# Weight pairs prepared in pieces, activations two items ahead, and a last pair without shared sums

## The chip, the cores and the metric

The kernel runs on one core of a Trainium2 chip. The metric is the device time of one execution in microseconds (us). A core has a matrix engine (TensorE, PE in the profile), a vector engine (VectorE, DVE), a scalar engine (ScalarE, ACT), GpSimd (POOL), and SyncE (SP), which here only starts transfers. Each works through its own instructions in the order in which they stand, and waits on semaphores for the others. Line numbers in this part and in the prediction (L714) are those of the kernel before.

## The reference

A transformer-like block on x of 2048 rows by 512 columns, all in float32. Six vectors of 512 come from a condition c. Then:

```
mod = (silu(c) @ w_mod)              # sa, ca, ga, sb, cb, gb
h = layernorm(x) * (1 + ca) + sa
x = x + ga * irfft2(rfft2(h) * (w_r + i w_i))
h = layernorm(x) * (1 + cb) + sb
a = mish(h @ w1 + b1)                # w1: 512 x 1376, mish(u) = u * tanh(softplus(u))
x = x + gb * (a @ w2)                # w2: 1376 x 512
```

## The kernel before

The work has four stages. Stages one and two do the forward transform, the product with the weights in the spectrum, and half of the way back. Stage three finishes the inverse transform, 16 row blocks of 128 rows each. The last stage is the MLP.

**Stage three** is a loop over s = 0 to 16, written out by hand: each engine gets its instructions in the order of the calls. A step has a column product (`p3_col`, L637 and L638, into a bank that ScalarE copies at L640), the row product of the step before (`p3_row`, L647, whose result VectorE adds to x at L650), and the statistics of that row block (`norm_sums`, L111 and L112). `norm_scale` (L116 and L117 on ScalarE, L124 and L129 on VectorE) turns the statistics of two or four row blocks into scales. Beside this the weights of the MLP are prepared. They are split into a high part in a shorter format and the rest, so that a product in float32 is made of three fast ones (`TERMS`). For w1: twelve pieces are loaded (L588), copied to the high part by ScalarE (L594) and subtracted by GpSimd (L595). For w2, in pairs t = 1 to 5 of 128 rows each, and a last odd piece t = 0 of 96 rows: `load_w2` (L673), `sum_w2` (GpSimd multiplies with the gate gb, L679, and forms four differences in `tsum`, L684), `split_w2` (ScalarE copies at L696, VectorE subtracts at L697). All of one function is called in one step; the table `prep` says in which. Pairs 4 and 5 are prepared after the loop, under the first MLP items.

**The MLP** goes over 8 blocks of two row blocks (b), each with 6 items (t). An item is the first product `up` (L714, 24 matmuls for a pair, 12 for t = 0, into one of two banks "A"), `mish` (ScalarE's Mish at L723, sums of halves on VectorE at L734, the high part `ah` by two copies of ScalarE at L740), `low` (the rest, `al`, VectorE at L746), and the second product `down` (L761; L755 for t = 0). For a pair, `down` multiplies a 2 x 2 scheme with 7 products of half size instead of 8; sums of weights (`tsum`) and of activations replace the eighth, and four of the results (`out_ps` banks 0, 3, 4, 5) are combined at the end of a block: `gather` copies them (L768), `chain` adds two of them up, `residual` adds banks 1 and 2 to x (L778), `spread` adds the combined ones (L783 to L787), `store` sends both row blocks out (L791). The tiles `ah` and `al` come from a pool with two buffers:

```
    act = ctx.enter_context(tc.tile_pool(name="act", bufs=2))
```

The next block's rows are normalised by `norm_pair` (ScalarE, L140) at t = 2, transposed by TensorE at t = 3 and 4 (`transpose_in`, L616, also into a bank "A") and split by `split_in` (L624 on ScalarE, L628 and L629 on VectorE). The step of item s is `up(s)`, `mish(s)`, `down(s - 1)`, `low(s)`.

Of the kernel before, what the change touches and what calls it, by code (L numbers as in the profile page):

```python
# [10 lines left out]
ALU = mybir.AluOpType  # L11

P = 128
# [12 lines left out]
LAST = (RAW[0], *SUM[0:3], RAW[1], RAW[2], SUM[3])  # L26
# [3 lines left out]
def tile_spectral_block(ctx: ExitStack, tc: tile.TileContext, x_d, w1_d, b1_d, w2_d,  # L30
# [645 lines left out]
    def sum_w2(t):  # L676
        rs = st["w2", t]
        for r in rs:
            nc.gpsimd.tensor_tensor(r, r, gbr[:r.shape[0]], op=ALU.mult)  # L679
        if t:  # L680
            u, v = rs
            for o, a, b in ((0, u[:, 256:], u[:, 0:256]), (1, v[:, 256:], tsum[:, 0]),
                            (2, v[:, 256:], u[:, 256:]), (3, v[:, 0:256], tsum[:, 1])):
                nc.gpsimd.tensor_tensor(tsum[:, o], a, b, op=ALU.subtract)  # L684

    def split_w2(t):
        rs = st.pop(("w2", t))
        hi, lo = w2[t]
        if t == 0:
            parts = [(rs[0], hi[:96], lo[:96])]  # L690
        else:
            flat = [w.rearrange("p e d -> p (e d)") for w in (hi, lo)]
            cut = ((rs[0][:, 0:256], 0, 256), (rs[1], 256, 768), (tsum.rearrange("p e d -> p (e d)"), 768, 1792))
            parts = [(r, flat[0][:, a:b], flat[1][:, a:b]) for r, a, b in cut]
        for r, h, l in parts:
            nc.scalar.copy(h, r)  # L696
            nc.vector.tensor_tensor(l, r, plain(h), op=ALU.subtract)  # L697
# [19 lines left out]
    def mish(g):  # L717
# [8 lines left out]
        if t == 0:  # L726
            parts = [(w[:rows, 0:256], slice(0, 2))]
        else:
# [19 lines left out]
    def down(g):  # L748
# [9 lines left out]
        for n, half, e, r in LAST if g == NB * NT - 1 else RAW + SUM:  # L758
            o = out[n][:, 0:256] if half is None else out[n][:, 256 * half:256 * half + 256]
            for i, (p, q) in enumerate(TERMS):  # L760
                nc.tensor.matmul(o, a[p][:, e], w2[t][q][:, r], start=(half is None and t == 1 and i == 0),  # L761
                                 stop=(t == 5 and i == 2 and (n, half) != (1, 0)))
# [13 lines left out]
    def residual(b):  # L776
        for n, ps in ((2 * b + 1, out_ps[b][1]), (2 * b, out_ps[b][2])):
            nc.vector.tensor_tensor(x[:, n, :], x[:, n, :], ps, op=ALU.add)  # L778

    def spread(b, ea, eb):  # L780
        p, q = done.pop(b)
        u, v = x[:, 2 * b + 1, :], x[:, 2 * b, :]
        ea.tensor_tensor(u, u, p, op=ALU.add)  # L783
        ea.tensor_tensor(v[:, 256:], v[:, 256:], p[:, 256:], op=ALU.add)
# [11 lines left out]
    def mlp(s):  # L796
        b, t = divmod(s, NT)
        nxt = 2 * b + 2 if b < NB - 1 else None
        if s < total:
            up(s)  # L800
# [197 lines left out]
```

## Time and profile before

| what | value |
|---|---|
| three runs | 427.13 us median (426.91 to 430.45) |
| profiled execution, its own time | 427.34 us |
| its span, first to last instruction | 425.3 us |
| mean granted clock of TensorE | 0.985 |
| busy: PE, DVE, ACT, POOL | 396.7, 259.7, 220.3, 145.8 us |
| from the first product of stage three to the last | 110.87 to 172.59 us |
| start of the last product, last start of an output transfer's pair | 415.42, 421.73 us |

The busy time of TensorE is an upper bound, since the ends of pipelined matmuls are modelled. What counts is where an engine that bounds a stage stands still, and who ended that. A row of the timeline has start, duration, engine, line, operation, output<-input, partitions x elements, the number of such instructions merged, and in brackets the idle time before it and who ended it.

### The profile page before, as it was taken

What the parts mean: (1) busy time and instruction counts of PE and PEld (TensorE: products, weight loads), DVE (VectorE), ACT (ScalarE), POOL (GpSimd) and SP (SyncE); (2) the same over time, 40 slices, a digit from 0 to 9 for tenths busy, and PEclk for the clock granted to TensorE, in tenths of its full rate; (3) what the DMA queues carried; (4) which work ended last, traced back from release to release, by engine and by line L of the source; (5) the groups of instructions that cost most, each with busy time, mean ns of one, the idle gap of its engine ahead of it and who ended that gap; (6) DMA issues with size and microseconds to landing.
All of it is one profiled execution on the core that took longest, in us unless ns stands there. A gap on an engine that the chain in (4) does not pass through costs nothing.

```text
span 425.3 us, 8110 instructions
## 1 busy us (share of the span) xinstructions
PE 396.7 (93%) x3161; PEld 384.1 (90%) x3161; DVE 259.7 (61%) x543; ACT 220.3 (52%) x495; POOL 145.8 (34%) x180
## 2 busy tenths in 40 slices
PE   9999899999977777899999999999999999999993
PEld 8888778899877776899999999999999999999993
DVE  2899949677166766779655455545644654563534
ACT  2677754577544443466464354454455553554431
POOL 0677625565075546415500500500500401303101
PEclk9999999999998969999999999999999999999998
DMA  8999652281203222010000100100100100100101
GB/s 300 379 337 363 219 208 75 76 324 50 74 18 117 66 99 62 26 51 2 17 34 2 46 5 2 51 1 2 52 2 0 51 2 0 51 2 0 51 2 49
DMA packets 20613, 34.72 MB, mean 82 GB/s; under 512 B 3680, under 2 KB 6528, under 8 KB 20192
## 3 DMA queue, kind: packets, MB, share of 16 engines
q1 hardware_dynamic: 20144, 33.68, 23.1%
q8 instruction: 25, 0.41, 0.4%
q10 hardware_dynamic: 432, 0.53, 0.4%
q14 instruction: 12, 0.10, 0.1%
HBM read 30.01 MB, written 4.19 MB: 80 GB/s over the span
## 4 chain that ended last, share of the span: by engine, by line
PE 64%; DVE 17%; ACT 6%; issue 5%; POOL 5%; DMA 2%; DVEq 0%; POOLq 0%; ACTq 0%
PE bank L714 26%; PE bank L761 20%; PE bank L455 3%; PE bank L755 3%; PE bank L501 3%; DVE st L111 3%; DMA buf<-in_B_w_dram 2%; POOL modr L684 2%; DVE ve L124 2%; POOL buf L679 2%; PE bank L488 2%; DVE buf L734 1%; PE bank L434 1%; DVE buf L226 1%; DVE buf L206 1%
## 5 line engine op out<-in xcount | busy, mean ns | idle before, releaser
L734 DVE TENSOR_TENSOR buf<-buf 128x128 f32<-128x128 f32 x160 | 52.2, 367 | 70.9 <-ACT buf L723 69.4
L723 ACT ACTIVATE buf<-bank,b1n 128x256 f32<-128x256 f32 (+1 forms) x88 | 37.3, 470 | 74.4 <-PE bank L714 74.4
L740 ACT CAST ah<-buf 128x512 fp32r<-128x512 f32 (+2 forms) x88 | 48.6, 552 | 38.7 <-DVE buf L734 37.1
L746 DVE TENSOR_TENSOR al<-buf,ah 128x512 fp32r<-128x512 f32 (+2 forms) x88 | 54.9, 624 | 10.0 <-ACT ah L740 10.0
L773 POOL TENSOR_TENSOR buf<-buf 128x256 f32<-128x256 f32 x7 | 5.2, 743 | 158.1 <-ACT buf L768 158.1
L714 PE MATMUL bank<-h2o,w1h 128*128 128x256 f32 (+1 forms) x352 | 52.8, 282 | 0.0
L714 PE MATMUL bank<-h,w1h 128*128 128x256 f32 (+1 forms) x352 | 52.7, 282 | 0.0
L714 PEld LDWEIGHTS bank<-h2o,w1h 128*128 128x128 f32 (+1 forms) x352 | 46.5, 186 | 0.3
L714 PEld LDWEIGHTS bank<-h,w1h 128*128 128x128 f32 (+1 forms) x352 | 46.4, 186 | 0.3
L761 PE MATMUL bank<-w2a,ah 128*128 128x256 f32 x168 | 36.8, 286 | 0.0
L761 PE MATMUL bank<-w2b,ah 128*128 128x256 f32 x168 | 36.3, 283 | 0.0
L647 PE MATMUL bank<-kiv,buf 128*128 128x128 f32 x128 | 19.3, 300 | 12.5 <-ACT buf L640 12.5
L647 PEld LDWEIGHTS bank<-kiv,buf 128*128 128x128 f32 x128 | 17.4, 211 | 13.5 <-ACT buf L640 13.5
L761 PEld LDWEIGHTS bank<-w2b,ah 128*128 128x128 f32 x168 | 28.2, 191 | 0.0
L761 PEld LDWEIGHTS bank<-w2a,ah 128*128 128x128 f32 x168 | 28.1, 191 | 0.0
L714 PE MATMUL bank<-h,w1l 128*128 128x256 f32 (+1 forms) x176 | 28.0, 282 | 0.0
L714 PE MATMUL bank<-h2o,w1l 128*128 128x256 f32 (+1 forms) x176 | 28.0, 282 | 0.0
L637 PE MATMUL bank<-kc,d 128*128 128x128 f32 x128 | 26.2, 288 | 0.5 <-ACT d L359 0.5
L638 PE MATMUL bank<-kc,d 128*128 128x128 f32 x128 | 26.0, 286 | 0.0
L233 PE MATMUL bank<-buf,mring 128*128 128x512 f32 x48 | 21.4, 445 | 4.2 <-DVE buf L226 1.9
L111 DVE BATCH_NORM_STATS2 st<-x 128x6 f32<-128x512 f32 x32 | 22.0, 688 | 3.8 <-DMA x<-in_A_x_dram 3.4
L595 POOL TENSOR_TENSOR w1l<-buf,w1h 128x512 fp32r<-128x512 f32 (+1 forms) x12 | 14.7, 1229 | 28.0 <-ACT w1h L594 28.0
(195 smaller groups left out, 1007.5 us busy)
## 6 DMA issues: line engine op xcount, KB each, us to landing
buf<-in_B_w_dram SPq DMA_DIRECT2D x18, 256.0 KB, 2.8
xring<-in_x_t_dram SPq DMA_DIRECT2D x16, 256.0 KB, 4.5
x<-in_A_x_dram SPq DMA_DIRECT2D x16, 256.0 KB, 4.8
wm<-in_w_mod_dram SPq DMA_DIRECT2D x16, 256.0 KB, 4.3
out_dram<-x SPq DMA_DIRECT2D x16, 256.0 KB, 2.0
mraw<-in_km_dram SPq DMA_DIRECT2D x16, 128.0 KB, 4.5
wqa<-in_w_q_dram SPq DMA_DIRECT2D x8, 256.0 KB, 4.4
wqb<-in_w_q_dram SPq DMA_DIRECT2D x8, 256.0 KB, 5.7
```

What stands on the lines that cost most here:

```text
L111: nc.vector.bn_stats(t, x[:, n, :])
L233: nc.tensor.matmul(pa, m[:, a, 0:128], g, start=(i == 0), stop=False)
L595: nc.gpsimd.tensor_tensor(w1l[:, k, lo:hi], r, plain(w1h[:, k, lo:hi]), op=ALU.subtract)
L637: nc.tensor.matmul(o, dj[:, 0:128], kc[0][:, n, :], start=True, stop=False)
L638: nc.tensor.matmul(o, dj[:, 64:192], kc[1][:, n, :], start=False, stop=True)
L647: nc.tensor.matmul(px[:, j * P:(j + 1) * P], e[:, j * P:(j + 1) * P], kiv[:, j, :], start=True, stop=True)
L714: nc.tensor.matmul(ps[:rows, 256 * e:256 * e + 256], w[:, k, f * P:f * P + rows], h[:, k, :], start=(i == 0), stop=(i == 11))
L723: nc.scalar.activation(w[:rows, c], ps[:rows, c], AF.Mish, bias=b1n[:rows, f:f + 1])
L734: nc.vector.tensor_tensor(o, p, q, op=op)
L740: nc.scalar.copy(h, r)
L746: nc.vector.tensor_tensor(l, r, h, op=ALU.subtract)
L761: nc.tensor.matmul(o, a[p][:, e], w2[t][q][:, r], start=(half is None and t == 1 and i == 0), stop=(t == 5 and i == 2 and (n, half) != (1, ...
```

## The change

- `sum_w2` becomes `gate_w2` (one tile at a time) and `sum_w2` (some of the differences); `split_w2` takes the raw part or the differences. For pairs 1, 2 and 3, starting at step s = 1, 6 and 11, the load stands at step s - 1, the two gate products at s and s + 1, the raw split and two differences at s + 2, the other two at s + 3, the split of the differences at s + 5. The order within a step and the steps of `norm_scale` and `norm_pair` are moved.
- `up(0)` stands at step 15 and `up(1)` at step 16 of stage three; `down` follows two items behind (`LAG = 2`). `norm_pair` moves to t = 3, the transpositions to t = 4 and 5 and ahead of `up`; the end of a block moves to t = 1.
- The last pair of the last block is multiplied plainly (8 products of half size, made as 4 of 512 columns, 12 matmuls), with raw weights that are loaded and gated once more. The shared sums are so complete one item earlier, and `finish` orders the end.

```
-LAST = (RAW[0], *SUM[0:3], RAW[1], RAW[2], SUM[3])
+LAG = 2
...
@@ -673,28 +673,40 @@
             nc.sync.dma_start(r, w2_d[f * P:f * P + rows, :])
             rs.append(r)
 
-    def sum_w2(t):
-        rs = st["w2", t]
-        for r in rs:
+    def gate_w2(t, *es):
+        for e in es:
+            r = st["w2", t][e]
             nc.gpsimd.tensor_tensor(r, r, gbr[:r.shape[0]], op=ALU.mult)
-        if t:
-            u, v = rs
-            for o, a, b in ((0, u[:, 256:], u[:, 0:256]), (1, v[:, 256:], tsum[:, 0]),
-                            (2, v[:, 256:], u[:, 256:]), (3, v[:, 0:256], tsum[:, 1])):
-                nc.gpsimd.tensor_tensor(tsum[:, o], a, b, op=ALU.subtract)
-
-    def split_w2(t):
-        rs = st.pop(("w2", t))
+
+    def sum_w2(t, *os):
+        u, v = st["w2", t]
+        for o in os:
+            a, b = ((u[:, 256:], u[:, 0:256]), (v[:, 256:], tsum[:, 0]),
+                    (v[:, 256:], u[:, 256:]), (v[:, 0:256], tsum[:, 1]))[o]
+            nc.gpsimd.tensor_tensor(tsum[:, o], a, b, op=ALU.subtract)
+
+    def split(h, l, r):
+        nc.scalar.copy(h, r)
+        nc.vector.tensor_tensor(l, r, plain(h), op=ALU.subtract)
+
+    def split_w2(t, sums):
         hi, lo = w2[t]
         if t == 0:
-            parts = [(rs[0], hi[:96], lo[:96])]
+            split(hi[:96], lo[:96], st.pop(("w2", 0))[0])
+            return
+        h, l = (w.rearrange("p e d -> p (e d)") for w in (hi, lo))
+        if sums:
+            split(h[:, 768:], l[:, 768:], tsum.rearrange("p e d -> p (e d)"))
         else:
-            flat = [w.rearrange("p e d -> p (e d)") for w in (hi, lo)]
-            cut = ((rs[0][:, 0:256], 0, 256), (rs[1], 256, 768), (tsum.rearrange("p e d -> p (e d)"), 768, 1792))
-            parts = [(r, flat[0][:, a:b], flat[1][:, a:b]) for r, a, b in cut]
-        for r, h, l in parts:
-            nc.scalar.copy(h, r)
-            nc.vector.tensor_tensor(l, r, plain(h), op=ALU.subtract)
+            u, v = st["w2", t]
+            split(h[:, 0:256], l[:, 0:256], u[:, 0:256])
+            split(h[:, 256:768], l[:, 256:768], v)
+
+    def plain_w2():
+        w2["plain"] = [w.rearrange("p e d -> p (e d)") for w in w2[1]]
+        h, l = w2["plain"]
+        for e, r in enumerate(st.pop(("w2", 5))):
+            split(h[:, 512 * e:512 * e + 512], l[:, 512 * e:512 * e + 512], r)
 
     def apply_gate():
         gb = bank("B")
@@ -725,6 +737,8 @@
         acts[g] = hi, lo
         if t == 0:
             parts = [(w[:rows, 0:256], slice(0, 2))]
+        elif g == total - 1:
+            parts = [(w, slice(0, 4))]
         else:
             u = buf("g2")
             a = w.rearrange("p (e s) -> p e s", s=P)
@@ -755,11 +769,19 @@
                     nc.tensor.matmul(out[n], a[p][:96, half], w2[0][q][:96], start=(i == 0), stop=False)
             return
         out = out_ps[b]
-        for n, half, e, r in LAST if g == NB * NT - 1 else RAW + SUM:
+        if g == total - 1:
+            for n, half in ((2, 0), (1, 1)):
+                for f in range(2):
+                    for i, (p, q) in enumerate(TERMS):
+                        nc.tensor.matmul(out[n], a[p][:, half + 2 * f], w2["plain"][q][:, 512 * f:512 * f + 512],
+                                         start=False, stop=(f == 1 and i == 2))
+            return
+        for n, half, e, r in RAW + SUM:
             o = out[n][:, 0:256] if half is None else out[n][:, 256 * half:256 * half + 256]
+            last = t == 5 or (half is None and g == total - 2)
             for i, (p, q) in enumerate(TERMS):
                 nc.tensor.matmul(o, a[p][:, e], w2[t][q][:, r], start=(half is None and t == 1 and i == 0),
-                                 stop=(t == 5 and i == 2 and (n, half) != (1, 0)))
+                                 stop=(last and i == 2 and (n, half) != (1, 0)))
 
     def gather(b):
         out = out_ps[b]
...
@@ -773,21 +795,29 @@
         eng.tensor_tensor(q[:, 0:256], q[:, 0:256], p[:, 0:256], op=ALU.add)
         eng.tensor_tensor(q[:, 256:], q[:, 256:], q[:, 0:256], op=ALU.add)
 
-    def residual(b):
-        for n, ps in ((2 * b + 1, out_ps[b][1]), (2 * b, out_ps[b][2])):
-            nc.vector.tensor_tensor(x[:, n, :], x[:, n, :], ps, op=ALU.add)
-
-    def spread(b, ea, eb):
-        p, q = done.pop(b)
+    def residual(b, rows=(1, 0)):
+        for r in rows:
+            n = 2 * b + r
+            nc.vector.tensor_tensor(x[:, n, :], x[:, n, :], out_ps[b][2 - r], op=ALU.add)
+
+    def rows_of(b):
+        p, q = done[b]
         u, v = x[:, 2 * b + 1, :], x[:, 2 * b, :]
-        ea.tensor_tensor(u, u, p, op=ALU.add)
-        ea.tensor_tensor(v[:, 256:], v[:, 256:], p[:, 256:], op=ALU.add)
-        eb.tensor_tensor(u[:, 256:], u[:, 256:], q[:, 0:256], op=ALU.add)
-        vv = v.rearrange("p (j d) -> p j d", j=2)
-        eb.tensor_tensor(vv, vv, q[:, 256:].unsqueeze(1).to_broadcast([P, 2, 256]), op=ALU.add)
-
-    def store(b):
-        for n in (2 * b + 1, 2 * b):
+        return (
+            lambda eng: eng.tensor_tensor(u, u, p, op=ALU.add),
+            lambda eng: eng.tensor_tensor(u[:, 256:], u[:, 256:], q[:, 0:256], op=ALU.add),
+            lambda eng: eng.tensor_tensor(v[:, 256:], v[:, 256:], p[:, 256:], op=ALU.add),
+            lambda eng: eng.tensor_tensor(v.rearrange("p (j d) -> p j d", j=2), v.rearrange("p (j d) -> p j d", j=2),
+                                          q[:, 256:].unsqueeze(1).to_broadcast([P, 2, 256]), op=ALU.add))
+
+    def spread(b):
+        chain(b, nc.gpsimd)
+        for fn in rows_of(b):
+            fn(nc.gpsimd)
+
+    def store(b, rows=(1, 0)):
+        for r in rows:
+            n = 2 * b + r
             nc.sync.dma_start(ov[:, n:n + 1, :], x[:, n:n + 1, :])
 
     total = NB * NT
@@ -796,31 +826,47 @@
     def mlp(s):
         b, t = divmod(s, NT)
         nxt = 2 * b + 2 if b < NB - 1 else None
-        if s < total:
-            up(s)
-        if t in (3, 4) and nxt:
-            transpose_in(nxt, t - 3)
-        parts = mish(s) if s < total else ()
-        if t == 2 and nxt:
+        if t in (4, 5) and nxt:
+            transpose_in(nxt, t - 4)
+        up(s)
+        if t in (4, 5) and nxt:
+            split_in(nxt, t - 4)
+        parts = mish(s)
+        if t == 3 and nxt:
             norm_pair(nxt)
-        down(s - 1)
-        if t == 0:
+        down(s - LAG)
+        if t == 1 and b:
             gather(b - 1)
-            if s == total:
-                chain(b - 1, nc.vector)
             residual(b - 1)
         low(parts)
-        if t in (3, 4) and nxt:
-            split_in(nxt, t - 3)
-        if t == 0:
-            if s < total:
-                chain(b - 1, nc.gpsimd)
-            spread(b - 1, nc.gpsimd, nc.vector if s == total else nc.gpsimd)
+        if t == 1 and b:
+            spread(b - 1)
             store(b - 1)
 
+    def finish():
+        b = NB - 1
+        down(total - 2)
+        gather(b)
+        own, ahead, far, both = rows_of(b)
+        chain(b, nc.vector)
+        far(nc.vector)
+        own(nc.gpsimd)
+        both(nc.vector)
+        down(total - 1)
+        residual(b, (0,))
+        store(b, (0,))
+        ahead(nc.vector)
+        residual(b, (1,))
+        store(b, (1,))
+
     apply_gate()
-    prep = {1: (load_w2, 1), 2: (sum_w2, 1), 3: (split_w2, 1), 4: (load_w2, 2), 5: (sum_w2, 2), 8: (split_w2, 2),
-            9: (load_w2, 3), 10: (sum_w2, 3), 11: (split_w2, 3), 12: (load_w2, 0), 13: (sum_w2, 0), 16: (split_w2, 0)}
+    prep = {s: [] for s in range(N2 + 1)}
+    for t, s in ((1, 1), (2, 6), (3, 11)):
+        for lag, fn, *args in ((-1, load_w2, t), (0, gate_w2, t, 0), (1, gate_w2, t, 1), (2, split_w2, t, False),
+                               (2, sum_w2, t, 0, 1), (3, sum_w2, t, 2, 3), (5, split_w2, t, True)):
+            prep[s + lag].append((fn, args))
+    prep[14].append((load_w2, (0,)))
+    prep[15].append((gate_w2, (0, 0)))
     for s in range(N2 + 1):
         if s < N2:
             p3_col(s)
@@ -828,37 +874,54 @@
             load_w1(s)
         if s >= 1:
             p3_row(s - 1)
+        if s in (3, 5):
+            norm_scale(s - 3, s - 1)
+        if s in (9, 13):
+            norm_scale(s - 5, s - 1)
+        if s == 15:
+            up(0)
+        if s == 16:
+            up(1)
         if s in (7, 8):
             transpose_in(0, s - 7)
+        if s >= 1:
+            norm_sums(s - 1)
         if 2 <= s < 14:
             split_w1(s - 2)
         if s in (8, 16):
             w2_space({8: 2, 16: 4}[s])
-        if s in prep:
-            prep[s][0](prep[s][1])
-        if s >= 1:
-            norm_sums(s - 1)
-        if s in (2, 4):
-            norm_scale(s - 2, s)
-        if s in (8, 12, 16):
-            norm_scale(s - 4, s)
-        if s == 4:
+        for fn, args in prep[s]:
+            fn(*args)
+        if s == 5:
             norm_pair(0)
         if s in (7, 8):
             split_in(0, s - 7)
-        if s == 16:
-            up(0)
-    low(mish(0))
+    norm_scale(N2 - 4, N2)
+    split_w2(0, False)
+    parts = mish(0)
+    low(parts)
+    parts = mish(1)
+    low(parts)
     load_w2(4)
-    sum_w2(4)
-    for s in range(1, total + 1):
+    gate_w2(4, 0, 1)
+    sum_w2(4, 0, 1, 2, 3)
+    for s in range(LAG, total):
         mlp(s)
-        if s == 2:
-            split_w2(4)
+        if s == 3:
+            split_w2(4, False)
+            split_w2(4, True)
             load_w2(5)
-            sum_w2(5)
-        if s == 4:
-            split_w2(5)
+            gate_w2(5, 0, 1)
+            sum_w2(5, 0, 1, 2, 3)
+        if s == 5:
+            split_w2(5, False)
+            split_w2(5, True)
+        if s == total - 5:
+            load_w2(5)
+            gate_w2(5, 0, 1)
+        if s == total - 3:
+            plain_w2()
+    finish()
 
 
 def _constants():
```

## The prediction

> **What bounds the kernel now.** I first read the busy time in four stretches: stage three (the inverse transform by columns and rows with the weights of the MLP prepared beside it), the first MLP items, the rest of the MLP, and the end. Columns: stretch, its length, then for each engine the busy time and the instructions, then the granted clock.
>
> ```profile
> 110.87:172.59 61.72, 49.19 (x392) 48.21 (x393) 37.93 (x72) 26.37 (x55) 33.99 (x32) 0.92 0.21 63
> 172.59:182.85 10.26, 9.03 (x69) 8.32 (x68) 7.61 (x17) 4.53 (x9) 4.37 (x5) 1.00 0.08 27
> 182.85:415.42 232.57, 232.11 (x1915) 230.17 (x1914) 128.11 (x289) 117.83 (x246) 46.06 (x48) 1.00 0.05 19
> 415.42:425.30 9.88, 2.97 (x23) 2.56 (x21) 4.41 (x8) 1.55 (x5) 1.94 (x2) 0.87 0.14 53
> ```
>
> The MLP is bound by TensorE: 232.11 of 232.57 us busy. Only there does every stall of TensorE count in full, and nothing that only makes another engine faster counts. TensorE loses time in stage three and in the 9.88 us from the start of the last product. The waits of stage three (waiter, who ended it; total, times, longest) say why:
>
> ```profile
> ACT rstd L116 <- DVE mv L112: 12.6, 5, 3.4
> PE bank L647 <- ACT buf L640: 12.5, 5, 4.7
> ACT w L696 <- POOL modr L684: 2.9, 1, 2.9
> ```
>
> The row product L647 waits for the copy L640, which stands on ScalarE behind the wide weight copy L696 (waiting for GpSimd's differences) or behind L116 (waiting for statistics that VectorE makes after the weights' low parts). A long wait costs twice, as the clock shows in stretches of 3.41 us:
>
> ```profile
> 129.24:132.65 3.41, 1.26 (x12) 1.07 (x10) 2.60 (x9) 1.97 (x5) 0.00 (x0) 1.00 0.69 219
> 132.65:136.06 3.41, 2.94 (x14) 2.94 (x15) 1.62 (x4) 1.93 (x4) 2.40 (x2) 0.50 0.09 19
> ...
> 146.30:149.71 3.41, 0.06 (x1) 0.00 (x0) 2.77 (x6) 0.93 (x4) 0.00 (x0) 1.00 0.20 53
> 149.71:153.13 3.42, 2.08 (x10) 2.08 (x10) 3.06 (x9) 2.67 (x6) 1.54 (x2) 0.50 0.00 0
> ...
> 159.95:163.37 3.42, 2.01 (x18) 1.81 (x17) 0.36 (x2) 1.10 (x2) 3.42 (x4) 1.00 0.00 0
> ```
>
> Each half-clock stretch follows one in which TensorE was busy 1.26 or 0.06 us; after 2.01 us there is none. So the limit lies between 37% and 59% of a stretch.
>
> **The change, part by part.**
>
> *Stage three.* Undisturbed, a step costs what lies between two row products:
>
> ```profile
> 117.23 1.06 PE L647 MATMUL bank<-kiv,buf 128*128 128x128 f32 x8
> ...
> 119.91 1.06 PE L647 MATMUL bank<-kiv,buf 128*128 128x128 f32 x8
> ```
>
> That is 2.68 us; 16 steps and two transpositions (0.35 us each, from 219.39 to 219.74 in the step shown below) make 43.6 us. The stage took 61.7, so 18.1 are lost. The first items (two first products, up(0) half-sized, one half-sized second product, another first product: 1.42 + 2.85 + 1.42 + 2.85 = 8.5 us) took 10.26: 1.7 more. In all 19.8 us can be won at most.
>
> The change spreads a weight pair over six steps: loads one step ahead, a gate product in each of two steps, narrow copies and two differences, two more differences, and the wide copy two steps later. That copy then finds its differences made, and the scale of the norms stands one step behind its statistics. GpSimd's work is the same, and the groups of instructions between 113 and 172 give its price (count | busy us, mean ns):
>
> ```profile
> L595 POOL TENSOR_TENSOR w1l<-buf,w1h 128x512 fp32r<-128x512 f32 x8 | 10.4, 1299 | 24.5 <-ACT w1h L594 24.5
> L679 POOL TENSOR_TENSOR buf<-buf,modr 128x512 f32<-128x512 f32 x7 | 8.8, 1271 | 2.6 <-DMA buf<-in_B_w_dram 2.6
> L684 POOL TENSOR_TENSOR modr<-buf,modr 128x256 f32<-128x256 f32 x6 | 5.1, 858 | 0.2
> ```
>
> A pair needs two gates (2.5), four differences (3.4) and five low parts of w1 (6.5 at most): 12.4 us in five steps of 13.4. It fits, with little to spare. On SP's queue the first w2 loads now stand ahead of w1's second piece, and later ones behind pieces whose buffer GpSimd has released; each lands more than a step before its use. I expect the five waits to go.
>
> One wait stays, behind the last row product. up(0) now runs before that product and up(1) after it, but up(2) needs up(0)'s bank, which the first Mish must read:
>
> ```profile
> 173.43 0.65 DVE L650 TENSOR_TENSOR x<-x,bank 128x512 f32<-128x512 f32 x1
> 174.61 0.68 DVE L111 BATCH_NORM_STATS2 st<-x 128x6 f32<-128x512 f32 x1
> 175.54 0.30 ACT L116 ACTIVATE rstd<-mv,eps 128x4 f32<-128x4 f32 x1 [3.40 <-DVE mv L112]
> 176.09 1.28 ACT L723 ACT_TABLE_LOAD   x1
> 177.39 0.47 ACT L723 ACTIVATE buf<-bank,b1n 96x256 f32<-96x256 f32 x1
> ```
>
> From L650 to L116 took 2.1 us, of which 0.5 was a weight part between them that now comes later; from L116 to the end of Mish 2.3; the copy of w2's last piece (512 columns, like L740's 0.62 below, less 0.1 of overlap), now between, adds 0.5; 0.2 passes before L650, as between TensorE and ScalarE below. So Mish ends 4.6 us after the row product, and up(1) covers 2.85: 1.8 us idle, taken as 2. With 0.5 at the start of the stage and 1.1 for waits of VectorE on GpSimd's work, 3.6 us stay lost: **gain 16.2**. Bounds: 17.3 if only the 2.5 us stay. On the other side stands how GpSimd's work beside VectorE stretches it; the same instruction took
>
> ```profile
> 140.58 1.65 DVE L629 TENSOR_TENSOR h<-buf,h 128x512 fp32r<-128x512 f32 x1
> ...
> 151.01 0.69 DVE L629 TENSOR_TENSOR h<-buf,h 128x512 fp32r<-128x512 f32 x1
> ```
>
> with GpSimd at work (L595) and without. VectorE's five steps hold some 11 us of such work; if much of it is stretched, row products wait again and 8 us are lost: gain 11.8. I take the value near the upper bound, since in most rows of the stage (0.68 to 0.69) nothing is stretched.
>
> *Two items ahead.* Nothing is won by this in the MLP, where TensorE never waits. But two things move together. There are two buffers for the activations ah and al, unchanged. The copy into ah of item s must now wait for the product of item s-2, which the order puts *behind* up(s). And the transpositions of the next pair of rows move from behind up at t=3 to *ahead of* up at t=4, while norm_pair moves from t=2 to t=3. One step of before, for the durations:
>
> ```profile
> 216.54 0.64 PE L714 MATMUL bank<-h2o,w1h 128*128 128x256 f32 x4
> 219.39 0.60 PE L616 MATMUL bank<-ident,buf 128*128 128x128 f32 x4
> 219.74 0.48 PE L761 MATMUL bank<-w2a,ah 128*128 128x256 f32 x2
> 222.33 0.64 PE L714 MATMUL bank<-h2o,w1h 128*128 128x256 f32 x4
> ...
> 216.68 1.52 ACT L140 ACTIVATE buf<-x,nmr,rstd 128x512 f32<-128x512 f32 x2
> 219.59 0.84 ACT L723 ACTIVATE buf<-bank,b1n 128x256 f32<-128x256 f32 x2 [1.39 <-PE bank L714]
> 220.46 0.51 ACT L740 CAST ah<-buf 128x384 fp32r<-128x384 f32 x1
> 221.51 0.62 ACT L740 CAST ah<-buf 128x512 fp32r<-128x512 f32 x1 [0.54 <-DVE buf L734]
> ```
>
> Before, norm_pair (L140, at 216.7) was done 1.2 us before its transposition L616 came up at 219.4. After, TensorE's order at t=3 and 4 is up(3), down(1), L616, up(4). ScalarE's is Mish(3), two copies into ah, two L140. Let X be the end of down(1). Its 21 matmuls stand 0.12 apart and the last reads al, so the last read of ah lies 0.12 earlier; ScalarE starts 0.2 us after what it waited for (219.39 to 219.59): X + 0.1. The copies take 0.51 + 0.62 less 0.1 overlap, the two L140 1.52 and start 0.1 early: X + 2.55. The transpositions wait for them, up(4) behind them, and TensorE has nothing else: with one of the four transpositions done in between, **2.5 us idle**. Blocks 0 to 6 have it: **17.5 us**. Bounds: 1.6 a block if the buffers did not hold the copies up (in the step shown L140 would then run from 222.04 to 223.56, and the product would end at 222.0), so 11.2; 2.7 if nothing overlaps, so 18.9.
>
> *Clock.* A stall of 2.5 us leaves 0.9 us of work when it lies in one 3.41 us stretch, under the 1.26 that brought the half clock. Straddling two, neither falls low enough unless 1.7 to 2.0 us fall in one. A block with its stall lasts about 33.1 us (five items of 2.85 + 2.55, one of half that, 0.7 for transpositions, 2.5), 9.7 stretches, so the place shifts back 1.1 us from block to block, and forward some 0.5 after a half-clock stretch (1.7 us longer). Walking through that, 4 to 6 of 7 stalls are punished; each costs half of 3.41 less what is idle anyway, 1.6: **7.5 us**, between 0 and 11.2.
>
> [...]
>
> *The end.*
>
> ```profile
> 416.04 0.37 ACT L768 COPY buf<-bank 128x256 f32<-128x256 f32 x1 [0.38 <-PE bank L761]
> 417.27 0.95 ACT L768 COPY buf<-bank 128x256 f32<-128x256 f32 x3 [0.86 <-PE bank L761]
> 417.67 0.43 DVE L773 TENSOR_TENSOR buf<-buf 128x256 f32<-128x256 f32 x1 [1.29 <-ACT buf L768]
> 418.65 1.28 DVE L778 TENSOR_TENSOR x<-x,bank 128x512 f32<-128x512 f32 x2
> 419.48 1.26 POOL L783 TENSOR_TENSOR x<-x,buf 128x512 f32<-128x512 f32 x1 [24.02 <-DVE x L778]
> 420.78 0.93 DVE L785 TENSOR_TENSOR x<-x,buf 128x256 f32<-128x256 f32 x1 [0.84 <-POOL x L783]
> 421.63 0.68 DVE L787 TENSOR_TENSOR x<-x,buf 128x512 f32<-128x512 f32 x1
> 421.73 0.94 SPq L791 DMA_DIRECT2D out_dram<-x  x2
> ```
>
> From the start of the last product (415.42) to the end 9.88 us pass. Now the shared sums are complete one product earlier, so gather, chain and row sums run under the last one. From its start: the four copies done at 1.5 (0.25 + 0.37 + 0.95), chain and far (0.43 each, the first beside the copies) to 2.4, both (0.68) to 3.1, first residual (0.68) 3.85, ahead (0.43) 4.35, second residual 5.05; own (1.26 on GpSimd) is beside them; then 3.0 for the store (422.31 to the end), 8.05. TensorE's twelve products of 512 columns, at twice 0.12, end before 3.2 and cost nothing. **Gain 1.8** (1.0 to 2.3). The second load and gating of w2's last pair (two transfers, two gates of 1.27, four narrow splits) stands behind the stores and row sums of block 6 and is asked for four items before the last product uses it, over 20 us of TensorE's work that hide it; without that cover the 2.5 us of gates would show.
>
> **The sum.** The profiled execution took 427.34 us (span 425.3), 0.2 above the median of the three runs: 427.34 - 16.2 + 17.5 + 7.5 - 1.8 = **434.3 us**.
>
> **Rivals.** *No half clock*: the stalls stay, but too much work lies beside them, 434.3 - 7.5 = 426.8. For it: a stretch with 1.4 us idle (159.95) was followed by full clock. Against: one with 2.15 us idle (129.24) was not, and 2.5 is more. [...] *The buffers do not hold the copies up*: 427.34 - 16.2 - 1.8 + 11.2 = 420.5, faster; against it stand the two buffers and the order. *The transposition is not late at all*: 409.3; it would need L140 ahead of the copies. *Preparation still stalls stage three*: slower still, by GpSimd's 12.4 of 13.4 us and the stretching at L629; from about 0.3 us more per step the row products wait. Gain 11.8 or less: 438.7 to 441.
>
> **How the numbers follow.** Forecast 0.70 (own range 430.0 to 438.5: 4 to 6 punished stalls and the terms' nearer bounds), no half clock 0.12, buffers 0.06, no lateness 0.03, stalled preparation 0.09. This kernel's runs tell 1% from nothing, that is 422.9 and 431.4. Slower: 0.09 and 0.63 of the forecast's 0.70, 0.72; the same: 0.12 and the forecast's lower edge, 0.07, 0.19; faster: 0.06 + 0.03, 0.09. The range reaches from 426.0, which takes in no half clock, to 441.0.
>
> **What would show it.** Right: L616 waiting for ScalarE's L140 seven times, about 2.5 us each, with half-clock stretches after most; L647 without waits in stage three; the last row product near 156; the last store issued some 5 us after the last product's start. Wrong: MLP blocks still 30.5 us apart, or waits at L647 above 5 us in all.

## The result, and the profile after

The kernel after takes 440.18 us (median of four runs, 438.18 to 441.96), the kernel before 427.92 (426.91 to 430.45): a ratio of 1.0276, 95% interval 1.021 to 1.0342, slower. The profiled execution of after took 439.86 us, its span 438.0, at a mean granted clock of 0.970 (before: 427.34, 425.3, 0.985). So 12.5 us have to be found. One execution of all that are reported here, the profiled one of experiment 9, ran at about half speed throughout (772.77 us; the 24 matmuls of a first product in 5.56 us, not 2.85) and is left out.

The same four stretches as before: from the start of stage three to the end of the last row product (up(0) now lies ahead of that), to the point where three first products and one second product are done, to the start of the last product, and the rest.

```profile
110.66:159.34 48.68, 45.92 (x404) 45.37 (x405) 40.45 (x71) 26.02 (x54) 33.12 (x30) 1.00 0.26 74
159.34:171.05 11.71, 8.93 (x57) 8.48 (x56) 8.97 (x20) 5.92 (x13) 5.82 (x6) 0.85 0.18 47
171.05:429.91 258.86, 243.79 (x1915) 239.30 (x1913) 143.82 (x287) 114.78 (x248) 52.16 (x52) 0.96 0.06 19
429.91:438.00 8.09, 2.91 (x14) 2.07 (x12) 4.57 (x7) 0.49 (x2) 1.42 (x1) 0.87 0.17 65
```

The three first products and the second one are done at 171.05, where they were done at 182.85: 11.8 us won. The MLP from there takes 258.86 where it took 232.57: 26.3 lost, with the same 1,915 matmuls in the records, some of them at half clock (a granted clock of 0.50). The end takes 8.09, not 9.88: 1.8 won. Together the span grows by 12.7.

TensorE's waits of after (waiter, who ended it; total, times, longest):

```profile
PE bank L616 <- ACT buf L140: 15.1, 14, 1.8
PE bank L726 <- ACT buf L735: 2.8, 1, 2.8
...
PE bank L647 <- DVE ve L124: 1.6, 1, 1.6
...
PE bank L647 <- ACT buf L640: 0.6, 1, 0.6
...
PE bank L647 <- DVE x L650: 0.5, 1, 0.5
```

The row products L647 wait 2.7 us in all, where they waited 12.5 for L640 alone. Two waits are new: the transpositions L616, seven pairs of waits, and one first product (L726, up(2)). One stall of L616, in order of time:

```profile
176.54 1.03 ACT L754 CAST ah<-buf 128x384 fp32r<-128x384 f32 x2 [1.61 <-PE bank L783]
177.48 1.51 ACT L140 ACTIVATE buf<-x,nmr,rstd 128x512 f32<-128x512 f32 x2
178.34 0.33 PE L616 MATMUL bank<-ident,buf 128*128 128x128 f32 x1 [1.78 <-ACT buf L140]
179.05 0.55 PE L616 MATMUL bank<-ident,buf 128*128 128x128 f32 x3 [0.38 <-ACT buf L140]
179.35 0.76 PE L726 MATMUL bank<-h,w1h 128*128 128x256 f32 x4
...
180.77 1.91 PE L726 MATMUL bank<-h,w1h 128*128 128x256 f32 x8
```

ScalarE waits 1.61 us for the product L783 that still reads ah, copies, normalizes two row blocks, and TensorE waits for these. Behind it eight matmuls take 1.91 us, where at 172.00, at full clock, they took 1.11. The stall costs 2.59 us a block (33.06 from block to block when nothing else is lost, by the third experiment, against 30.47 before). The blocks of after, from one up(3) to the next, stand 34.57, 34.58, 34.57, 34.37, 33.05, 34.58 and 34.54 apart: six of the seven stalls lost another 1.3 to 1.5 us to the clock, and are called punished below. Cut into stretches of 3.41 us (from 176.46 here, from 129.24 in before, and on from there both ways), the traces of after and before show every stretch wholly at a granted clock of 1.00 or wholly at 0.50. That at the kernels' ends aside, half clock lasted one stretch each time in after, and in before one (from 132.65) and two (6.83 us, from 149.71). Around three of the stalls:

```profile
176.46:179.87 3.41, 1.26 (x9) 0.96 (x9) 1.66 (x4) 3.33 (x7) 0.00 (x0) 1.00 0.00 0
179.87:183.29 3.42, 3.42 (x18) 3.42 (x17) 2.93 (x4) 1.81 (x3) 0.77 (x1) 0.50 0.53 153
...
278.86:282.27 3.41, 1.63 (x13) 1.36 (x12) 2.87 (x8) 2.01 (x4) 0.00 (x0) 1.00 0.20 77
282.27:285.69 3.42, 3.04 (x15) 2.92 (x15) 0.89 (x2) 1.47 (x3) 0.00 (x0) 0.50 0.00 0
...
312.99:316.41 3.42, 1.67 (x14) 1.46 (x13) 3.10 (x8) 1.99 (x5) 0.00 (x0) 1.00 0.20 77
316.41:319.82 3.41, 3.01 (x24) 2.82 (x25) 1.01 (x2) 1.70 (x3) 0.00 (x0) 1.00 0.00 0
```

After 1.26 or 1.63 us of matmuls the next stretch runs at half clock; the stall at 316.43 lies across two stretches, the first with 1.67, and goes unpunished.

The first items. From the last row product's end at 159.34:

```profile
159.17 0.66 DVE L650 TENSOR_TENSOR x<-x,bank 128x512 f32<-128x512 f32 x1
...
160.69 0.66 DVE L650 TENSOR_TENSOR x<-x,bank 128x512 f32<-128x512 f32 x1
161.38 0.69 DVE L111 BATCH_NORM_STATS2 st<-x 128x6 f32<-128x512 f32 x1
...
162.33 0.30 ACT L116 ACTIVATE rstd<-mv,eps 128x4 f32<-128x4 f32 x1 [2.94 <-DVE mv L112]
...
162.77 0.60 ACT L689 CAST w2b<-buf 96x512 fp32r<-96x512 f32 x1
...
164.68 0.47 ACT L735 ACTIVATE buf<-bank,b1n 96x256 f32<-96x256 f32 x1
...
165.21 0.74 PE L726 MATMUL bank<-h,w1h 128*128 128x256 f32 x4 [2.78 <-ACT buf L735]
```

VectorE adds the last row at 160.69, 1.35 us after its product ended, since it is still at the row before. Everything behind it, down to Mish and up(2), is as much later.

### The profile page after: what moved, and what is told of

It reads as the page before. It is cut to its first block, busy times and chain, and to the rows that moved or that the text cites. A ratio compares the mean times of both kernels' runs of the same rounds, so it can differ in the third digit from the quotient of the medians.

```text
span 438.0 us, 8143 instructions
## 1 busy us (share of the span) xinstructions
PE 404.8 (92%) x3152; PEld 389.9 (89%) x3152; DVE 279.2 (64%) x541; ACT 217.2 (50%) x496; POOL 152.5 (35%) x181
## 4 chain that ended last, share of the span: by engine, by line
PE 69%; DVE 19%; ACT 7%; issue 2%; DMA 1%; POOL 1%; SPq 0%; ACTq 0%; DVEq 0%; POOLq 0%
PE bank L726 30%; PE bank L783 22%; DVE st L111 4%; PE bank L455 3%; PE bank L501 3%; PE bank L769 3%; DVE ve L124 2%; ACT buf L140 2%; PE bank L616 2%; DVE x L650 2%; ACT ah L754 2%; PE bank L488 2%; DMA x<-in_A_x_dram 1%; PE bank L434 1%; DVE buf L226 1%
## 5 line engine op out<-in xcount | busy, mean ns | idle before, releaser
L760 DVE TENSOR_TENSOR al<-buf,ah 128x512 fp32r<-128x512 f32 (+2 forms) x87 | 64.0, 759 | 38.1 <-ACT ah L754 38.1
L754 ACT CAST ah<-buf 128x512 fp32r<-128x512 f32 (+2 forms) x87 | 45.3, 552 | 80.5 <-PE bank L783 48.5
L726 PE MATMUL bank<-h,w1h 128*128 128x256 f32 (+1 forms) x352 | 57.5, 298 | 2.8 <-ACT buf L735 2.8
L726 PE MATMUL bank<-h2o,w1h 128*128 128x256 f32 (+1 forms) x352 | 56.3, 294 | 0.0
L726 PEld LDWEIGHTS bank<-h,w1h 128*128 128x128 f32 (+1 forms) x352 | 50.3, 202 | 3.3 <-ACT buf L735 3.0
L726 PEld LDWEIGHTS bank<-h2o,w1h 128*128 128x128 f32 (+1 forms) x352 | 49.5, 198 | 0.3
L783 PE MATMUL bank<-w2a,ah 128*128 128x256 f32 x168 | 36.3, 283 | 0.0
L783 PE MATMUL bank<-w2b,ah 128*128 128x256 f32 x161 | 34.4, 283 | 0.0
L726 PE MATMUL bank<-h,w1l 128*128 128x256 f32 (+1 forms) x176 | 30.1, 297 | 0.0
L726 PE MATMUL bank<-h2o,w1l 128*128 128x256 f32 (+1 forms) x176 | 29.3, 291 | 0.0
L783 PEld LDWEIGHTS bank<-w2a,ah 128*128 128x128 f32 x168 | 28.1, 191 | 0.0
L783 PEld LDWEIGHTS bank<-w2b,ah 128*128 128x128 f32 x161 | 26.9, 192 | 0.0
L616 PE MATMUL bank<-ident,buf 128*128 128x128 f32 x64 | 12.7, 307 | 15.1 <-ACT buf L140 15.1
L679 POOL TENSOR_TENSOR buf<-buf,modr 128x512 f32<-128x512 f32 (+1 forms) x13 | 17.2, 1329 | 26.2 <-DMA buf<-in_B_w_dram 14.3
L726 PEld LDWEIGHTS bank<-h,w1l 128*128 128x128 f32 (+1 forms) x176 | 25.8, 202 | 0.0
L637 PE MATMUL bank<-kc,d 128*128 128x128 f32 x128 | 24.8, 276 | 0.5 <-ACT d L359 0.5
L726 PEld LDWEIGHTS bank<-h2o,w1l 128*128 128x128 f32 (+1 forms) x176 | 25.2, 197 | 0.0
```

Source lines behind the costliest of these rows:

```text
L616: nc.tensor.transpose(ps[:, (2 * k + i) * P:(2 * k + i + 1) * P], h[:, (2 * g + k) * P:(2 * g + k + 1) * P], ident)
L637: nc.tensor.matmul(o, dj[:, 0:128], kc[0][:, n, :], start=True, stop=False)
L726: nc.tensor.matmul(ps[:rows, 256 * e:256 * e + 256], w[:, k, f * P:f * P + rows], h[:, k, :], start=(i == 0), stop=(i == 11))
L760: nc.vector.tensor_tensor(l, r, h, op=ALU.subtract)
```

## The experiments

Each kernel ran beside the kernel before on the same chip, whose medians there were 427.87, 428.21 and 428.14 us in the three groups. Ratios are to these, with 95% intervals.

**1. The transposition behind the first product** (e1_behind; edit to after):

```diff
-        if t in (4, 5) and nxt:
-            transpose_in(nxt, t - 4)
         up(s)
+        if t in (4, 5) and nxt:
+            transpose_in(nxt, t - 4)
```

> The changed kernel with one edit: the transpositions of the next rows stand behind up at t = 4 and 5 instead of ahead of it. Theory (the seven stalls come from the transpositions meeting norm_pair too early; from the first whole item to the last product the changed kernel spends 26.3 us more than the kernel before): L140 then has the 2.85 us of up to finish in, no wait at L616, no half clock in the MLP, 440.2 - 26.3 = 413.9 us. Rival (the two activation buffers alone make the items late, wherever the transpositions stand): stalls move to other products, about 430 or more.

Measured: 414.34 us (412.42 to 415.52), ratio 0.9667 (0.9631 to 0.9704). Two exchanged calls give 26 us back (414.34 against the 440.18 of after). The MLP takes 233.43 us, 25.4 less than in after, at full clock:

```profile
172.19:405.62 233.43, 232.35 (x1914) 230.16 (x1913) 143.46 (x287) 115.00 (x248) 52.64 (x52) 1.00 0.06 21
405.62:413.70 8.08, 2.91 (x14) 2.08 (x12) 4.58 (x7) 0.49 (x2) 1.44 (x1) 0.99 0.17 65
```

So stalls and half clock both hang on the place of L616 against L140.

**2. A third buffer for ah** (e2_buf3):

```diff
-        hi, lo = (act.tile([P, 7, P], F32R, name=n) for n in ("ah", "al"))
+        hi, lo = (act.tile([P, 7, P], F32R, name=n, bufs=k) for n, k in (("ah", 3), ("al", 2)))
```

> The changed kernel with three buffers for ah (al keeps two), so that the copies into ah no longer wait for the product of two items before. Theory: norm_pair starts about 1 us earlier, the stall shrinks from 2.6 to 1.5 us a block (10.5 to 11 in all) and becomes too short for the half clock, so 440.2 - 26.3 + 11 = 425 us. Rival (the copies do not wait for the buffer): nothing changes, 440. Rival (the half clock comes at 1.5 us as well): 432.

Measured: 425.64 us (425.26 to 426.66), ratio 0.995 (0.9931 to 0.9969). The copies no longer wait for the product, and L140 comes earlier, but not early enough:

```profile
208.95 0.62 ACT L754 CAST ah<-buf 128x512 fp32r<-128x512 f32 x1 [0.69 <-DVE buf L748]
209.48 1.51 ACT L140 ACTIVATE buf<-x,nmr,rstd 128x512 f32<-128x512 f32 x2
210.34 0.33 PE L616 MATMUL bank<-ident,buf 128*128 128x128 f32 x1 [0.98 <-ACT buf L140]
```

The copy now waits for VectorE's sums. From the second block on the blocks stand 32.3 to 32.4 us apart, 1.9 more than before, and half clock follows only the first stall. That bears out the buffers as the reason for 0.7 us of the 2.59, and leaves the rest to the order.

**3. Work in the stall** (e3_fill; ahead of the first transposition of each pair):

```diff
+        if n and g == 0:
+            for _ in range(18):
+                nc.tensor.matmul(ps[:, 0:256], w1h[:, 0, 0:P], h2[n // 2 - 1][0][:, 0, :], start=True, stop=True)
```

> The changed kernel with 18 extra products of 256 columns (2.1 us, their result is overwritten and not used) ahead of the first transposition of each block, that is inside the stall of 2.6 us. Theory (half clock by the work inside stretches of 3.41 us costs some 8 us of the 26.3): stalls last as long as before, counted with the extra products, but no half clock follows them: 440.2 - 8 = 432 us, faster by added work. Rival (the clock costs nothing here, the stall alone is longer than thought): 440 or more.

Measured: 430.11 us (429.79 to 430.5), ratio 1.0051 (1.0036 to 1.0067). The 126 added products, whose result is overwritten, make the kernel 10 us faster than after. They fill the stalls: the transposition (L619 here) waits 1.5 us for L140 in all, where it waited 15.1:

```profile
208.99 2.32 PE L615 MATMUL bank<-h2o,w1h 128*128 128x256 f32 x18
...
211.63 0.55 PE L619 MATMUL bank<-ident,buf 128*128 128x128 f32 x3 [0.21 <-ACT buf L140]
```

The seven blocks are all 33.06 us apart; the only half clock left ahead of the kernel's end follows the wait of up(2):

```profile
161.24:164.65 3.41, 0.74 (x7) 0.53 (x5) 2.83 (x8) 2.71 (x5) 0.62 (x1) 1.00 0.01 2
164.65:168.06 3.41, 3.31 (x15) 3.31 (x16) 2.33 (x7) 2.32 (x6) 1.10 (x1) 0.50 0.32 82
```

**4. The changed preparation alone** (e4_stage): the kernel before with the diff's parts of stage three (prep, norm_scale, norm_sums, norm_pair(0), the split functions), and not its order of items, LAG or finish.

> The kernel before with the changed preparation of stage three alone (pieces over six steps, scales one step later); the MLP one item ahead and the end are as before. Theory: stage three loses 3.7 us instead of 18.1, and the first items lose what they lost before: 427.9 - 14.4 = 413.5 us. Rival (the stage is only faster because the first products of items 0 and 1 fill it): the waits at L647 come back in part, 418 or more.

Measured: 415.38 us (415.1 to 415.7), ratio 0.9707 (0.9692 to 0.9722): this part wins 12.5 us by itself, some 2 less than expected. Its longest waits in stage three and behind it are two for VectorE and one for ScalarE's copy into ah:

```profile
PE bank L647 <- DVE x L650: 1.9, 1, 1.9
PE bank L761 <- ACT ah L746: 1.8, 1, 1.8
PE bank L647 <- DVE ve L124: 1.7, 1, 1.7
```

**5. The last scale and the copy of w2's last piece out of the way of Mish** (e5_late_scale; edit to 1):

```diff
-    norm_scale(N2 - 4, N2)
-    split_w2(0, False)
     parts = mish(0)
+    split_w2(0, False)
     low(parts)
...
         mlp(s)
+        if s == 12:
+            norm_scale(N2 - 4, N2)
```

> The kernel after with the transpositions behind the first product, and the scale of the last four rows' norms (L116 and what follows) moved out from between the last row product and the first Mish to the third block, where ScalarE has time; the copy of w2's last piece stands behind that Mish. My theory: the 2.7 us for which up(2) waits are the chain L650, L111, L112, L116, copy, table load, Mish; without its first five links Mish is done before up(1) ends, the wait goes and with it the half clock that follows it in some executions: 412.4 (the fastest execution with the wait) less 2.7 is 409.7 us, no wait above 0.5 us at up(2). Rival: the wait only passes to another engine (VectorE's low parts for the first second product): 411.5 us or more, with a wait of 2 us at L769.

Measured: 412.16 us (411.06 to 413.47), ratio 0.9626 (0.9602 to 0.9651). The wait of up(2) is gone, with the half clock: the first second product starts at 165.51, in the first experiment at 170.46. The wait of 2 us at L769 that the rival asked for is not there. But of the 4.6 us that the expectation asked for against the median of 1, 2.2 came out. The expectation had started from the fastest execution of 1, 412.42, and the four of 1 reach from there to 415.52. In the two profiled executions (415.52 and 411.66) up(3) starts 4.7 us sooner after the start of stage three, and 1.4 us of that are lost again later:

```profile
161.10 0.47 ACT L735 ACTIVATE buf<-bank,b1n 96x256 f32<-96x256 f32 x1
...
175.69 0.55 PE L616 MATMUL bank<-ident,buf 128*128 128x128 f32 x3 [0.32 <-ACT buf L140]
184.89 0.48 PE L726 MATMUL bank<-h2o,w1h 128*96 128x256 f32 x2 [0.37 <-ACT buf L624]
239.08 0.55 PE L616 MATMUL bank<-ident,buf 128*128 128x128 f32 x3 [0.38 <-ACT buf L140]
```

In the first block ScalarE's work on the next pair (L140, L624) is a little late, and behind the moved scale, which needs three table loads of 1.28 us there, L140 is late once more. A wait of 0.97 us for L628, which stands behind VectorE's weight parts, is in experiment 1 as well.

**6. The old end** (e6_old_end; edit to 1): no second load of the pair and no plain_w2, the last product in the order LAST, and

```diff
     def finish():
         b = NB - 1
         down(total - 2)
+        down(total - 1)
         gather(b)
         own, ahead, far, both = rows_of(b)
         chain(b, nc.vector)
-        far(nc.vector)
+        residual(b)
         own(nc.gpsimd)
-        both(nc.vector)
-        down(total - 1)
-        ...
+        far(nc.gpsimd)
+        ahead(nc.vector)
+        both(nc.vector)
+        store(b)
```

> The kernel after with the transpositions behind the first product, and the end of before: the last pair as 21 products of 256 columns, then gather, chain, residuals, row sums, stores; no second load of the pair. My theory: 9.9 us from the start of the last product to the end in place of 8.1, so 1.8 us slower than the same kernel with the new end: 416.1 us. Rival: the second load, its gates and copies cost TensorE something in the last block, so that less than 0.8 us of the gain is left: 415.1 or less.

Measured: 415.27 us (414.29 to 417.45), ratio 0.9705 (0.9674 to 0.9736), 0.9 above experiment 1 and between the two expectations; the intervals of the two ratios overlap, so these times do not settle it. The profile is sharper:

```profile
406.32 0.28 PE L775 MATMUL bank<-w2c,ah 128*128 128x256 f32 x1
...
412.13 0.94 SPq L813 DMA_DIRECT2D out_dram<-x  x2
```

From the last product at 406.32 to the end at 415.7 it is 9.38 us. So of the 1.8 that the end won, 1.3 come from the last pair and its finish (9.38 to 8.08), and 0.5 from the order two items ahead, under which the activations of the last product are ready before it starts (9.88 to 9.38).

**7. Without the differences** (e7_no_sums; edit to 1): sum_w2 left out for the pairs 1 to 3.

> The kernel after with the transpositions behind the first product; left out are GpSimd's four differences of the first three weight pairs (L686; the copies then read what stands in that buffer). Theory A: what is lost in stage three (3.7 us) and at up(2) (2.7) comes from VectorE, whose work is stretched while GpSimd works beside it; with 10 us of GpSimd's work gone, the wait of L647 for L124 (1.8 us) goes, up(2) waits 1.5 us, 411.3 us. Theory B: VectorE is late because of the order of its own work (low parts ahead of a row's addition); the waits stay within 0.3 us, and 414.0 us.

Measured: 412.05 us (408.9 to 412.58), ratio 0.9598 (0.9559 to 0.9637), 2.3 us below experiment 1; the two intervals just overlap.

```profile
PE bank L726 <- ACT buf L735: 2.7, 1, 2.7
...
PE bank L647 <- ACT buf L640: 1.5, 1, 1.5
```

Neither theory holds whole. The wait of L647 for L124 is gone, but that alone says little, since experiment 6 has none either, with the differences in place. The sum says more: L647 waits 1.5 us in all, and 2.7 to 4.2 us in each of the ten traces that have the changed preparation with its differences. And VectorE's own rows are shorter: the low part of a weight (L690, w2a from buf and w2hi, 128x512) took 1.23 us in experiment 1 and 0.69 here. So in stage three GpSimd's work does make VectorE late. The wait of up(2) is the same 2.7 us: there it is VectorE's own queue, with the last row's addition behind the one before, and the whole chain of the scale ahead of Mish, without which (experiment 5) there is no such wait.

**8. norm_pair an item earlier** (e8_early_norm; edit to after):

```diff
-        if t == 3 and nxt:
+        if t == 2 and nxt:
             norm_pair(nxt)
```

> The kernel after with one line changed: norm_pair at t=2, where before has it, not t=3; the transpositions stay ahead of the first product. My theory: the stall is only that L140 is late, by its place behind the copies that wait for the product two items back; an item earlier it is done 5 us ahead, and 413.9 us, as with the transpositions behind the product. Rival: the place ahead of the first product is itself too early (the transposition's bank or ScalarE's reading of it is late as well): 425 us or more.

Measured: 413.35 us (412.57 to 414.67), ratio 0.9656 (0.9635 to 0.9677). TensorE never waits in the MLP, though the transpositions stand ahead of the first product; in the first block L140 ends at 175.26 and the transposition starts at 176.79, 1.5 us later and not the expected 5:

```profile
171.56:403.45 231.89, 231.89 (x1914) 229.97 (x1913) 145.47 (x286) 114.58 (x248) 52.43 (x52) 1.00 0.06 22
```

The place ahead of up(4) is harmless by itself; only the pair that it needs was late.

**9. Both edits, 8 and the late scale of 5** (e9_early_late).

> The kernel after with norm_pair at t=2 and with the scale of the last four rows' norms in the third block: both edits that each took a wait away. With norm_pair alone up(2) waited 2.75 us and a half-clock stretch followed (1.7); with the late scale alone two transpositions and one first product waited 1.0 us in all for work on ScalarE and VectorE that was late behind the table loads of the moved scale, which a pair normalized an item earlier does not feel. My theory: the two gains add, 413.35 - 2.75 - 1.7 = 408.9 us, blocks 30.5 apart throughout. Rival: the moved scale (4.3 us of ScalarE with three table loads) still makes something late in the third block and the low parts at the start of the MLP still hold the first block up: 411 us or more.

Measured: ratio 0.9592 (0.9566 to 0.9617); five executions between 409.55 and 412.39 us, median 410.82, the lowest of all versions. Of the expected 4.5 us over experiment 8, 2.5 came. The only trace of this kernel is of the execution that is left out, so where the other 2 stay is open; late work at the start of the MLP, as in 5, would fit.

**10 and 11. Four or two products in the stall** (e10_fill4, e11_fill2): as 3, with range(4) and range(2).

> The kernel after with four more matmuls of 256 columns (0.5 us; a product that is overwritten) on TensorE ahead of the first transposition, inside its stall. In the kernel after stretches of 3.41 us with 1.26 to 1.63 us of matmuls were followed by half clock, one with 1.67 was not. My theory: the limit lies between, so the stall that left 1.26 leaves 1.7 and no half clock follows any of the seven; the blocks are 33.06 us apart, as with eighteen such matmuls, and the time is 430.1 us. Rival: eighteen helped because they left nearly no idle time; four change nothing that matters: half clock after five or six stalls as before, 438 us or more.

> As the run with four matmuls, with two (0.24 us). Stretches with a whole stall then hold 1.5 us of work, under 1.63. By the limit of 1.65 us half clock still follows most stalls that lie in one stretch: 436 us or more, blocks of 34.6 us in most places. If the limit were lower (1.3 to 1.5), 430 to 432 us.

Measured: with four 438.8 us (436.78 to 439.64), ratio 1.0257 (1.023 to 1.0284); with two 439.91 (438.52 to 440.82), ratio 1.0271 (1.0244 to 1.0298). With two it came as expected, five of seven stalls punished. With four my theory fell: four of the seven were still punished. In its profile:

```profile
209.03:212.44 3.41, 1.73 (x14) 1.34 (x13) 1.72 (x5) 2.51 (x5) 0.00 (x0) 1.00 0.04 14
212.44:215.85 3.41, 3.41 (x19) 3.41 (x18) 1.12 (x2) 0.97 (x2) 0.00 (x0) 0.50 0.00 0
...
379.69:383.11 3.42, 1.86 (x14) 1.46 (x13) 2.49 (x7) 2.39 (x4) 0.00 (x0) 1.00 0.20 77
```

1.73 us of recorded work were punished here, 1.86 were not; in after 1.67 had not been. Over all the traces, every stretch at full clock with up to 1.50 us of matmuls was followed by half clock, and none with 1.75 or more. Between these both happen: 1.70 was punished in experiment 11 and not in 12, and 1.56 was not in experiment 1 (the stretch at 143.90, in stage three). So the limit can't be read closer than between 1.50 and 1.75 us (44% and 51%), about half of a stretch. The ends of matmuls in the records are modelled, which may be why; that something beside the busy time counts is not ruled out. My 1.65 came from reading two rows too finely.

**12. The order and the end alone** (e12_order): the kernel after with the steps of before for prep, norm_scale, norm_sums and norm_pair(0).

> The kernel after with the weights' preparation and the norms' scale of stage three in the steps of before: the two-items-ahead order and the new end alone. If the change's parts are independent, before gains what the MLP lost and the end won: 427.3 + 26.3 - 1.8 = 451.8 us, less up to 3 us where up(0) and up(1), now ahead of and behind the last row product, fill waits of stage three: 449 to 452 us, L616 waiting seven times 2.6 us. Rival: part of the 26 us comes from what the changed preparation leaves behind (weight parts at the start of the MLP): below 446 us.

Measured: 449.85 us (448.77 to 452.09), ratio 1.0513 (1.0481 to 1.0544), as expected.

```profile
PE bank L616 <- ACT buf L140: 15.0, 14, 1.8
PE bank L647 <- ACT buf L640: 13.1, 5, 4.8
```

The stalls of L616 are the same 15.0 us without the changed preparation, and L647 has all the waits of before: the two parts of the change are separate mechanisms. In size they don't quite add: the preparation is worth 12.5 us alone (4) and 9.7 beside the new order (449.85 less 440.18). In stage three and the first items they do. From the start of stage three to the point where three first products and one second product are done, before takes 71.98 us and experiment 4 takes 59.30; this kernel takes 72.74 and after 60.39. That is 12.7 and 12.4 us, and up(0) and up(1) are not seen to fill waits of stage three. What differs in these two profiled executions is the clock behind the stalls: five of the seven are punished here, six in after, which is 1.5 us.

## Why the prediction was right, point by point

The forecast was slower, 434.3 us, between 426 and 441, by a stall for L140 in front of L616 with half clock behind it. The mechanism is shown: experiments 1 and 8 take it away in two ways, 2 takes away the part of the buffers, 3 the part of the clock. The size is less good: the time lies above the forecast's own range, 430.0 to 438.5, and only inside the outer one. By its terms, with before's profiled 427.34 as the base:

| term | predicted | measured |
|---|---|---|
| stage three and the first items | -16.2 | -11.8 |
| seven stalls | +17.5 | +18.1 (7 times 2.59) |
| half clock | +7.5 | +8.8 (blocks 26.97 longer than 7 times 30.47, less 18.1) |
| the end | -1.8 | -1.8 |
| what before's first block loses over the others, not lost in after | - | -0.7 (31.17 against 30.47, from one transposition to the next) |

The measured terms sum to 439.9; the profiled execution took 439.86.

*The mis-sized term* is the first, and in two steps of it. "1.1 for waits of VectorE on GpSimd's work": beside the 0.5 at the start, 3.2 us were lost in stage three (48.68 less 43.6 and the 1.42 of up(0), less 0.5; of these 0.6, 1.6 and 0.5 at L647, the rest in small pieces). "1.8 us idle, taken as 2" at up(2): the wait was 2.78, and the half clock behind it, which the working did not ask for there, cost another 1.8 (a clock of 0.85 over 11.71 us). The chain from the last row's addition to Mish was right link by link (1.6 expected and 1.64 measured from L650 to L116, 2.8 and 2.82 from there to the end of Mish); wrong was its start, 0.2 us after the product, where VectorE was 1.35 behind. The gain became the lower bound, 11.8, and the time that of the rival "preparation still stalls stage three" (438.7 to 441). That agreement is chance, since the rival is not what happened: L647 waits 2.7 us, not 8, and more than half of the 8.3 us lost lies at up(2).

*The stalls* were sized from the order of ScalarE's queue, 2.5 against 2.59 by the blocks; 2.16 of that stand in the records as waits (15.1 in seven). Without the wait for the buffer 1.6 a block was expected, and experiment 2 measured 1.9, where the copy waits for VectorE's sums in its place. *The half clock* followed six stalls, as many as the upper count of "4 to 6 of 7"; a punished one cost 1.3 to 1.5, not 1.6. The 7.5 was also a little under the middle of its own count, five times 1.6. The bounds of the limit, 37% and 59% of a stretch, were right for a stretch at full clock, and are 44% and 51% by the runs. But the prediction's "each half-clock stretch follows one in which TensorE was busy 1.26 or 0.06 us" passes over one: behind the stretch of before at 149.71, at half clock and busy for 2.08 us (61%), stands another at half clock, so there that much did not bring the full clock back; behind 2.94 us (at 132.65) it was back.

```profile
153.13:156.54 3.41, 3.41 (x17) 3.41 (x17) 1.59 (x4) 0.00 (x0) 0.81 (x2) 0.50 0.75 238
```

In after a stretch with 2.15 us idle, at 176.46, was followed by half clock. So the rival without half clock did not come; experiment 3, where it is taken away, shows what it would have been worth, 10 us.

*The end* came out at 1.8 through other rows. The addition "far" took 1.51 us beside GpSimd's L807, not 0.43, but the sums were finished a product earlier and the last residual ended 4.9 us after the last product's start (5.05 worked out):

```profile
430.67 1.51 DVE L809 TENSOR_TENSOR x<-x,buf 128x256 f32<-128x256 f32 x1
...
433.73 1.47 SPq L821 DMA_DIRECT2D out_dram<-x  x2
434.14 0.69 DVE L801 TENSOR_TENSOR x<-x,bank 128x512 f32<-128x512 f32 x1
```

Of the signs that were named, the stalls, the half clock and the last store came as told; the last row product came at 158.46, not near 156, and L647 did wait in stage three, 2.7 us.

## What to carry to other kernels

When work is moved ahead in one engine's order, go through the queue of the engine that feeds it and ask what now stands in front of the feeding instruction, and for which buffer that waits; here one line (norm_pair an item earlier) decided between 13% of a block lost and 3.4% of the kernel won. Price a stall of TensorE twice: its own length, and the half clock behind it. Here half clock over the next 3.41 us cost 1.3 to 1.5 us in the MLP; it followed every stretch at full clock with up to 1.50 us of matmuls and none with 1.75 or more. Where a chain starts behind an engine that is nearly full, start it from where that engine's queue will be, not from the event that feeds it.

## What was not expected of the hardware

That useless products can make a kernel faster: 18 of them in each stall, 2.3 us of TensorE's time, took 10 us off, since the half clock went. And that a limit read from two rows 0.04 us apart (1.63 punished, 1.67 not) did not hold in the next kernel (1.73 punished): in the records of these kernels, busy time tells what follows only outside 1.50 to 1.75 us.
